# Attention feeding a maxout FFN: immediate activation biases, another path for the first K and Q, and denominators issued apart from numerators

## The chip, the cores and the metric

The kernel runs on one core of a Trainium2 chip. TensorE (PE) multiplies, VectorE (DVE) and ScalarE (ACT) work elementwise, GpSimd (POOL) and SyncE (SP) here mainly issue DMAs. POOL's DMAs can cast fp32 to fp16 on the way. The metric is the device time of one execution in microseconds (us). The kernel before takes 356.96 us, the median of 13 runs from 353.17 to 360.54.

## The reference

```python
scores = (q @ k.T) / sqrt(64)              # q, k, v: 8 batches, 12 heads, 448 x 64
e = exp(scores - max)
attn = e / (sum(e) + exp(-max))            # softmax with one added to the denominator
x = (attn @ v)                             # heads side by side: 3584 x 768
h = maximum(maximum(x @ w1, x @ w2), x @ w3)
out = h @ w_out                            # 3584 x 768, weights 768 x 768
```

## The kernel before

Heads are taken in groups of four: 8 batches times 3 groups are 24 groups, numbered 0 to 23. Matrix work is in fp16. For each group Q and K (two halves of two heads) and V are loaded by POOL with a cast, Q and K are transposed into `qkT`, scores are multiplied into PSUM tiles `stp`, ACT takes their exponential into `eT` (first name `eTp`), a product with ones gives the denominators `den`, ACT makes the reciprocal as `rb = exp(-ln(den + 1/8) + ln 256)` in two ACTIVATEs over `lnd`, a product with V gives the numerators (`num` or `av`), and DVE multiplies both into `xT`, the transposed input of the FFN. A piece of the up-projection multiplies `xT` with one of three weights into `p_i`, and DVE folds it into `hT` with a maximum. The down-projection writes `op_ps`, which DVE scales into `o_sb` and SP stores.

The order is written out by hand. For the start there is a string of operations; from group 4 on a loop issues, per group, scores, the numerators of two groups before, denominators of the group before, and FFN pieces by a credit. The letters of the string that matter: `Cg` cast of the pair for group g, `Tg` both transposes on PE, `Sgp` scores and exponentials of part p (the queries are cut into 3 and 4 blocks of 64), `sgp` the last of them, `Agp` denominators and numerators, `M1` one piece of up-projection, `U V W` the three score visits of a whole group, `X5` copies for group 5 and its transpose by DMA on SP. Groups 1 to 4 are transposed on PE, from 5 on by DMA.

PSUM tiles of two banks (`stp`, `den`) rotate over three buffers and tiles of one bank (`trT`, `num`, `p_i`, `op_ps`) over two; each engine does its instructions in the order given. Group 0's K and Q come as fp32 over the hardware queues of SP and ACT and are cast by DVE. POOL's loads are issued in the order of the calls; each waits for the eighth before it to land, and a tile's load waits until its buffer is free (five for Q and K, six for V). Biases of the ACTIVATEs are [128, 1] tiles that DVE sets once (`e_b`, `one_b`, `ln_lam`).

## Time and profile before

| | us |
|---|---|
| median of 13 runs | 356.96 |
| the profiled execution, whole | 355.06 |
| its span, first to last instruction | 353.3 |
| PE busy | 322.9 |
| DVE busy | 234.7 |
| ACT busy | 205.6 |
| POOL busy | 92.0 |
| first scores on PE | 11.91 |
| first up-projection on PE | 29.32 |
| scores of group 5 on PE, the first that wait for a transpose by DMA | 65.32 |

The profile is one execution. Busy time counts instructions that an engine is at; a busy PE is not PE at its peak. The page gives busy shares in slices, the granted PE clock, DMA traffic and the chain of work that ended last; tables by stage show which engine is full where. What counts for the time is the engine or the transfer that others wait for in a stage. Line numbers (L296) are those of the kernel before.

### The profile page before, as it was taken

Reading aid. Unit: us, or ns where it says so; the run is one execution under the profiler, and the core shown is the slowest. Engines: PE = TensorE matmul, PEld = TensorE weight load, DVE = VectorE, ACT = ScalarE, POOL = GpSimd, SP = SyncE. Lnnn points to the kernel's source line nnn. Section 1 sums busy time; section 2 is a strip of 40 time slices with the busy share of each in tenths; the row PEclk is TensorE's granted clock in tenths of the full one; section 3 lists DMA queues with packets and bytes.
Section 4 is the critical chain, followed back from the end, with each engine's and each line's share of the span. In section 5 each row is a group of like instructions: output and inputs, shape, how many; then the busy total and the mean of one; then the engine's idle time right before and its main releaser. Section 6 shows DMA issues by size and latency. Waiting matters only on the chain.

```text
span 353.3 us, 7731 instructions
## 1 busy us (share of the span) xinstructions
PE 322.9 (91%) x3198; PEld 180.7 (51%) x3198; DVE 234.7 (66%) x434; ACT 205.6 (58%) x226; POOL 92.0 (26%) x158
## 2 busy tenths in 40 slices
PE   0777879799999999999999999999999999899994
PEld 0656757454454554445445555455445544444552
DVE  0422458488677787787786777778777786654553
ACT  1598778588566667659458567566666665420000
POOL 6934957134240440342142143041000000000000
PEclk9999999899999999999999999999999999999999
DMA  8999999979955896598683995578302630022006
GB/s 162 194 209 205 184 202 166 139 113 228 134 90 95 151 186 106 78 121 153 124 126 65 182 186 92 90 125 167 65 8 54 163 70 2 0 66 69 0 4 177
DMA packets 63172, 41.93 MB, mean 119 GB/s; under 512 B 38048, under 2 KB 59552, under 8 KB 63136
## 3 DMA queue, kind: packets, MB, share of 16 engines
q0 software_dynamic: 23424, 20.78, 40.0%
q1 hardware_dynamic: 39424, 20.19, 27.3%
q10 hardware_dynamic: 288, 0.46, 0.6%
q8 instruction: 25, 0.41, 0.5%
q14 instruction: 11, 0.09, 0.1%
HBM read 42.47 MB, written 11.01 MB: 151 GB/s over the span
## 4 chain that ended last, share of the span: by engine, by line
PE 78%; ACT 8%; DMA 6%; DVE 5%; issue 1%; POOL 0%; SPq 0%; DVEq 0%
PE p_i L355 42%; PE op_ps L398 15%; PE av L238 8%; PE stp L198 7%; DVE xT L277 3%; PE p_i L376 3%; ACT eT L216 3%; DMA qkT<-qk 3%; ACT eTp L296 3%; DMA first_k<-in_k_dram 2%; PE den L238 2%; DMA ld_q<-in_q_dram 1%; ACT rb L327 1%; ACT lnd L323 1%; PE trT L168 1%
## 5 line engine op out<-in xcount | busy, mean ns | idle before, releaser
L216 ACT ACTIVATE eT<-stp,e_b 128x896 f16<-128x896 f32 x147 | 136.6, 1008 | 84.6 <-PE stp L198 84.6
L355 PE MATMUL p_i<-xT,w 128*128 128x448 f16 x756 | 148.1, 352 | 3.2 <-DVE xT L277 1.2
L355 PEld LDWEIGHTS <-w 128*128 128x128 f16 x756 | 72.7, 98 | 74.6 <-issue 9.6
L365 DVE TENSOR_TENSOR hT<-hT,p_i 128x448 f16<-128x448 f16 x84 | 52.2, 621 | 30.1 <-PE p_i L355 30.1
L224 DVE TENSOR_TENSOR eS<-eS,eT 128x896 f16<-128x896 f16 x105 | 65.0, 619 | 2.8
L88 POOL DMA_DIRECT2D ld_v<-in_v_dram x48 | 28.7, 609 | 137.7 <-PE stp L198 116.2
L198 PE MATMUL stp<-qkT 64*64 64x448 f16 (+2 forms) x756 | 53.7, 347 | 8.1 <-ACT eT L216 2.3
L398 PE MATMUL op_ps<-w,hT 128*128 128x384 f16 x336 | 57.8, 326 | 0.0
L398 PEld LDWEIGHTS <-hT 128*128 128x128 f16 x336 | 31.7, 98 | 24.6 <-issue 2.5
L405 DVE TENSOR_SCALAR o_sb<-op_ps 128x384 f32<-128x384 f32 x56 | 31.1, 555 | 15.2 <-PE op_ps L398 13.8
L198 PEld LDWEIGHTS <-qkT 64*64 64x64 f16 x756 | 21.4, 109 | 33.8 <-issue 28.1
L363 DVE CAST hT<-p_i 128x448 f16<-128x448 f32 x42 | 26.2, 625 | 17.4 <-PE p_i L355 17.4
L238 PE MATMUL av<-eT,ld_v 64*64 64x448 f16 x588 | 36.9, 362 | 0.9 <-DVE o_sb L405 0.5
L277 DVE TENSOR_TENSOR xT<-av,rb 128x448 f16<-128x448 f32 x42 | 24.3, 620 | 12.1 <-PE av L238 12.0
L238 PEld LDWEIGHTS <-ld_v 64*64 64x64 f16 x756 | 25.7, 108 | 12.8 <-issue 7.6
L88 POOL DMA_DIRECT2D ld_k<-in_k_dram x46 | 28.5, 642 | 5.2 <-DMA w<-in_moe_w_dram 3.3
L88 POOL DMA_DIRECT2D ld_q<-in_q_dram x46 | 28.1, 628 | 4.8 <-DMA w<-in_moe_w_dram 2.9
L296 ACT ACTIVATE eTp<-stp,e_b 128x768 f16<-128x768 f32 (+3 forms) x24 | 20.1, 910 | 11.0 <-PE stp L198 10.8
L257 ACT ACTIVATE lnd<-den,one_b 128x896 f32<-128x896 f32 x21 | 21.2, 1007 | 8.8 <-PE den L238 8.8
L376 PE MATMUL p_i<-xT,w 128*128 128x192 f16 (+1 forms) x216 | 22.8, 259 | 1.2 <-DVE xT L339 0.7
L259 ACT ACTIVATE rb<-lnd,ln_lam 128x896 f32<-128x896 f32 x21 | 21.9, 1042 | 0.7
L376 PEld LDWEIGHTS <-w 128*128 128x128 f16 x216 | 19.1, 98 | 5.4 <-issue 3.3
(36 smaller groups left out, 107.9 us busy)
## 6 DMA issues: line engine op xcount, KB each, us to landing
out_dram<-o_sb SPq DMA_DIRECT2D x56, 192.0 KB, 3.1
ld_v<-in_v_dram POOLq DMA_DIRECT2D x48, 112.0 KB, 4.1
ld_k<-in_k_dram POOLq DMA_DIRECT2D x46, 112.0 KB, 4.9
ld_q<-in_q_dram POOLq DMA_DIRECT2D x46, 112.0 KB, 4.6
w<-in_moe_w_dram POOLq DMA_DIRECT2D x3, 576.0 KB, 10.6
w<-in_moe_w_dram POOLq DMA_DIRECT2D x6, 288.0 KB, 9.8
w<-in_moe_w_out_dram POOLq DMA_DIRECT2D x3, 384.0 KB, 7.5
first_k<-in_k_dram SPq DMA_DIRECT2D x2, 224.0 KB, 6.0
```

The source lines that it names most:

```text
L88: eng.dma_start(out=dst[hp * KC : hp * KC + KC].rearrange("p s j d -> p s (j d)"), in_=src[:, half_heads(name, hp)],)
L198: nc.tensor.matmul(out=out[half(c), r], lhsT=qkT[half(r), 0, j, h], rhs=qkT[half(r), 1, q0:q1, h], start=True, stop=True,)
L216: nc.scalar.activation(out=st["eT"][:, j], in_=stp[:, :, 0:S], func=AF.Exp, scale=scale, bias=e_b)
L224: nc.vector.tensor_tensor(out=st["eS"], in0=st["eT"][:, 0] if j == 1 else st["eS"], in1=st["eT"][:, j], op=ALU.add,)
L238: nc.tensor.matmul(out=outs[r][half(c)], lhsT=weights(r, c), rhs=moving(r, c), start=start, stop=stop,)
L277: nc.vector.tensor_tensor(out=xT[b][:, 2 * g + r, :], in0=banks[r][:, 0:S], in1=st["rb"][:, r], op=ALU.mult)
L296: nc.scalar.activation(out=eT[:, j0 : j0 + n].rearrange("p j r q -> p r j q"), in_=stp[:, :, 0 : n * nq].rearrange("p r (j q) -> p r j q", ...
L355: nc.tensor.matmul(out=p_i[:, 0:S], lhsT=w_sb[i][:, dc, ts(fc, 128)], rhs=xT[b][:, dc, :], start=(dc == 0), stop=(dc == NDC - 1),)
L365: nc.vector.tensor_tensor(out=dst, in0=dst, in1=p_i[:, 0:S], op=ALU.max)
L376: nc.tensor.matmul(out=p_i[:, ts(j, nq)], lhsT=w_sb[i][:, dc, ts(2 * fp + j, 128)], rhs=xT[b][:, dc, q0 * KC : q1 * KC], start=(dc == 0), ...
L398: nc.tensor.matmul(out=op_ps[:, 0:NW], lhsT=hT[bp][:, fc, ts(t, 128)], rhs=wout_sb[:, fc, ts(nh, NW)], start=(fc == 0), stop=(fc == NFC - 1),)
L405: nc.vector.tensor_scalar(out=o_sb[:, ts(nh, NW)], in0=op_ps[:, 0:NW], scalar1=1.0 / LAMBDA, scalar2=None, op0=ALU.mult,)
```

## The change

- The three bias tiles and their memsets go; the ACTIVATEs take their biases as numbers in the instruction.
- Group 0's K comes in two halves, one on SP's and one on ACT's hardware queue. Group 0's Q is loaded by POOL's casting queue, first of POOL's loads, and is transposed like the other groups' (14 transposes of 64 rows in place of 7). Q's cast on DVE goes.
- POOL builds the identity ahead of group 1's loads instead of behind them. Among later loads the third weight goes ahead of group 3's K and Q, and group 3's V ahead of group 4's K and Q.
- V has five buffers instead of six.
- In the start, scores are issued one PSUM tile at a time (`Sgpu`, unit u), and `A` is split into `D` (denominators with the two ACTIVATEs) and `N` (numerators and the product on DVE), in another order.

```diff
-                [128, 2, NJ, D], MMDT, tag="ld_" + name, name="ld_" + name, bufs=6 if name == "v" else 5
+                [128, 2, NJ, D], MMDT, tag="ld_" + name, name="ld_" + name, bufs=5
...
-    first = {}
-    for name, eng in (("k", nc.sync), ("q", nc.scalar)):
-        first[name] = cpool.tile([128, 2, NJ, D], FP32, name="first_" + name)
-        for hp in range(2):
-            load_half(eng, first[name], name, 0, hp)
-    load_group(1, "kq")
+    first_k = cpool.tile([128, 2, NJ, D], FP32, name="first_k")
+    load_half(nc.sync, first_k, "k", 0, 0)
+    load_half(nc.scalar, first_k, "k", 0, 1)
+    load_group(0, "q")
     ident16 = cpool.tile([128, 128], MMDT, name="ident16")
     make_identity(nc, ident16)
+    load_group(1, "kq")
...
-            if i == 0:
+            if i == 0 and n == 0:
...
-                out=st["eT"][:, j], in_=stp[:, :, 0:S], func=AF.Exp, scale=scale, bias=e_b
+                out=st["eT"][:, j], in_=stp[:, :, 0:S], func=AF.Exp, scale=scale, bias=-math.log(EDIV)
...
+    load_weight(2)
     load_group(3, "kq")
-    load_weight(2)
+    load_group(3, "v")
     load_group(4, "kq")
-    load_group(3, "v")
...
-        C0 T0 S00 T1 s00 S10 T2 s10 A00 S20 A10 s20 S01 A20 s01
-        S11 M1 s11 M1 M1 A01 S21 M1 s21 M1 T3 M1 A11 U3 M1 A21 V3 T4 E30 M1 M1 W3 E31 X5 F
+        C00 T0 S000 S001 S002 T1 S003 S100 S101 D00 T2 S102 S103 N00 S200 S201 D10 S202 S203 N10
+        S010 D20 S011 S012 N20 S013 M1 M1 S110 D01 S111 N01 S112 S113 M1 M1 S210 D11 S211 N11
+        S212 S213 M1 T3 M1 D21 M1 U3 N21 T4 V3 E30 M1 M1 W3 E31 X5 F
```

What POOL's queue holds first, before (the names end in buffer numbers; ld_k_97 and ld_q_100 are group 1's, ld_v_108 is group 0's V):

```order
L88 DMA ld_k_97<-in_k_dram 64x2x448 x2
L88 DMA ld_q_100<-in_q_dram 64x2x448 x2
masks.py:197 MEMSET ident16_103 128x128
masks.py:199 ISA
masks.py:199 AFFINE_SELECT ident16_103<-ident16_103 128x128
L88 DMA ld_v_108<-in_v_dram 64x2x448 x2
```

And in the changed kernel (ld_q_94 is group 0's Q, ld_k_102 and ld_q_105 group 1's):

```order
L88 DMA ld_q_94<-in_q_dram 64x2x448 x2
masks.py:197 MEMSET ident16_97 128x128
masks.py:199 ISA
masks.py:199 AFFINE_SELECT ident16_97<-ident16_97 128x128
L88 DMA ld_k_102<-in_k_dram 64x2x448 x2
L88 DMA ld_q_105<-in_q_dram 64x2x448 x2
L88 DMA ld_v_108<-in_v_dram 64x2x448 x2
```

Group 0's Q has come in front, and group 1's K and Q have moved behind the identity.

ACT up to the third reciprocal, before (eTp 128x2x2x192 and 128x384 are exponentials of part 0, 128x2x2x256 of part 1):

```order
L296 ACTIVATE eTp<-stp,e_b 128x2x2x192 x3
L296 ACTIVATE eTp<-stp,e_b 128x384
L296 ACTIVATE eTp<-stp,e_b 128x2x2x192 x3
L296 ACTIVATE eTp<-stp,e_b 128x384
L323 ACTIVATE lnd<-den,one_b 128x2x192
L327 ACTIVATE rb<-lnd,ln_lam 128x2x192
L296 ACTIVATE eTp<-stp,e_b 128x2x2x192 x3
L323 ACTIVATE lnd<-den,one_b 128x2x192
L327 ACTIVATE rb<-lnd,ln_lam 128x2x192
L296 ACTIVATE eTp<-stp,e_b 128x384
L296 ACTIVATE eTp<-stp,e_b 128x2x2x256 x3
L323 ACTIVATE lnd<-den,one_b 128x2x192
```

And the end of the same stretch in the changed kernel, from the second reciprocal on:

```order
L307 ACTIVATE lnd<-den 128x2x192
L311 ACTIVATE rb<-lnd 128x2x192
L284 ACTIVATE eTp<-stp 128x2x2x192
L284 ACTIVATE eTp<-stp 128x384
L284 ACTIVATE eTp<-stp 128x2x2x256
L307 ACTIVATE lnd<-den 128x2x192
L311 ACTIVATE rb<-lnd 128x2x192
L284 ACTIVATE eTp<-stp 128x2x2x256 x2
```

The bias operands are gone, and one exponential of part 1 stands ahead of the third pair `lnd`, `rb` where there were three.

## The prediction

> **What bounds the kernel now.** I read the page's busy shares first, then a table of the engines by stage, then the chain that ended last over the first 60 us, the waits of PE, and single rows where a price was needed. Columns of the stage table: stretch, length, busy us (instructions) of PE, weight loads, DVE, ACT, POOL, then granted PE clock, DMA share, GB/s.

> ```profile
> span 353.3 us, 7731 instructions
> PE 322.9 (91%) x3198; PEld 180.7 (51%) x3198; DVE 234.7 (66%) x434; ACT 205.6 (58%) x226; POOL 92.0 (26%) x158
> ...
> 0.00:10.00 10.00, 0.48 (x5) 0.48 (x6) 1.30 (x6) 1.28 (x1) 7.34 (x17) 1.00 0.88 167
> 10.00:20.00 10.00, 8.87 (x204) 7.53 (x202) 3.76 (x7) 7.00 (x10) 7.51 (x13) 1.00 1.19 197
> 20.00:30.00 10.00, 6.08 (x186) 4.39 (x177) 1.87 (x6) 9.94 (x15) 4.39 (x8) 1.00 1.18 207
> 30.00:40.00 10.00, 9.56 (x178) 8.05 (x177) 4.69 (x9) 7.62 (x9) 6.19 (x11) 1.00 1.20 198
> 40.00:50.00 10.00, 8.14 (x194) 7.03 (x192) 3.86 (x10) 7.21 (x9) 6.25 (x11) 1.00 1.16 193
> 60.00:100.00 40.00, 36.43 (x346) 20.56 (x346) 29.07 (x55) 27.84 (x31) 10.69 (x18) 0.96 0.96 144
> 100.00:150.00 50.00, 49.51 (x427) 25.48 (x421) 38.81 (x73) 33.63 (x36) 14.26 (x24) 1.00 0.71 122
> ```

> The reader is to see three limits. From 100 us on PE has work for 49.5 of each 50 us: nothing off PE can gain there. From 20 to 30 us ACT is busy 9.94 of 10 and PE waits for it. Before 10 us nothing computes, and DMA is full at about 200 GB/s until past 50 us. So the change can only act in the first 65 us or so, and the chain there says where:

> ```profile
> 1.56 7.18 DMA first_k<-in_k_dram
> ...
> 8.84 0.64 DVE qk L147
> ...
> 9.52 1.69 PE trT L162 x14
> ...
> 11.23 0.64 DVE qkT L171
> ...
> 11.91 1.18 PE stp L198 x24
> ...
> 55.77 9.51 DMA qkT<-qk
> ```

> The first scores start at 11.91 because the second half of the first K lands at 8.74. At 55.77 the chain goes through the first DMA transpose (group 5).

> **The change, part by part.** *First loads.* Before, SP issues both K halves, ACT both Q halves, all fp32; POOL's first load is group 1's K.

> ```profile
> 0.74 1.65 SPq L88 DMA_DIRECT2D first_k<-in_k_dram  x2
> 0.77 1.37 ACTq L88 DMA_DIRECT2D first_q<-in_q_dram  x2
> 1.25 1.32 POOL L88 DMA_DIRECT2D ld_k<-in_k_dram  x2 [0.80 <-POOLq L570]
> 2.54 1.22 POOL L88 DMA_DIRECT2D ld_q<-in_q_dram  x2
> ...
> DMA to landing us min/median/max: 4.9/6.0/7.2
> DMA to landing us min/median/max: 3.9/4.8/5.7
> DMA to landing us min/median/max: 4.9/5.7/6.6
> ...
> ld_k<-in_k_dram POOLq DMA_DIRECT2D x46, 112.0 KB, 4.9
> first_k<-in_k_dram SPq DMA_DIRECT2D x2, 224.0 KB, 6.0
> ...
> 13.77 0.96 PE L168 MATMUL trT<-ident,ld_q 128*64 128x128 f16 x14
> ```

> The three landing rows are those of first_k, first_q and the first two ld_k. The 7.2 is the second K half, so SP's first landed at 0.74 + 4.9 = 5.64 and ACT's first at 0.77 + 3.9 = 4.67. In the changed kernel K's halves are these two firsts: K is there at 5.64. With the gaps of the chain (0.10 to the cast, 0.68 to the transposes, half of 1.69 for 7 of 14) K's transposes end at 7.26. Q now takes the place of ld_k: halves at 1.25 + 4.9 = 6.15 and about 1.97 + 6.6 = 8.57. Its 14 narrower transposes take 0.96, the copy 0.64, hand-overs 0.14. If Q is there by 7.26 the scores start at 8.95 (gain 2.97); at 8.57, at 10.3 (gain 1.6). Q's second half then no longer shares with 0.46 MB of fp32 Q, but still with K; I take 7.6, scores at 9.34: **-2.6**, ends -3.0 and -1.6. Three DVE memsets and one DVE cast go at a time when DVE only waits for K: nothing.

> POOL now builds the identity after Q, so group 1's K and Q are issued some 1.9 us later, where ld_q and ld_v stood. Rows like ld_q's (2.54, 3.16, landing 6.3) put their last half near 10.6. They are wanted at 10.5 and 11.4: the wait is 0 to 0.2, taken as 0. If that cover is gone (first scores before 9), it eats what was gained beyond.

> *Order of the first groups.* ACT sets the pace until the first up-projection:

> ```profile
> 12.50 3.17 ACT L296 ACTIVATE eTp<-stp,e_b 128x768 f16<-128x768 f32 x4 [10.47 <-PE stp L198]
> ...
> 23.65 3.58 ACT L296 ACTIVATE eTp<-stp,e_b 128x384 f16<-128x384 f32 x4
> 27.10 0.59 ACT L323 ACTIVATE lnd<-den,one_b 128x384 f32<-128x384 f32 x1
> 27.73 0.61 ACT L327 ACTIVATE rb<-lnd,ln_lam 128x384 f32<-128x384 f32 x1
> ...
> 29.32 1.16 PE L376 MATMUL p_i<-xT,w 128*128 128x192 f16 x12
> ```

> The chain to p_i is ACT back to back from 12.50 to rb's end at 28.34, then xT and PE. The row at 23.65 holds one exponential of 384 and three of part 1 (1024 wide); ahead of the third reciprocal the new order keeps one of the three. Two go: (3.58 - 0.52) / 3 = 1.02 each, -2.04. Against it stands a new ACT gap: T2 is put ahead of S102, and group 1's exponentials wait for it, taken as 0.45 (after S101 PE needs about 3.1 at the early rows' pace for denominators, transposes and S102; ACT has about 2.65 to do). Net **-1.6** (ends -2.0 and -0.6). The two exponentials are done later, where ACT is 7.6 and 7.2 of 10 busy: hidden while that slack of 5.2 stands. From 30 to 50 PE is idle 0.44 + 1.86 = 2.3; much of it stands behind numerators whose reciprocal comes late, and denominators issued earlier should take some: **-0.5** (ends 0 and -1.8). The same nine pieces of up-projection are issued by the end of the start, so behind it the program is unchanged.

> *Immediates.* Each ACTIVATE loses the read of a [128,1] bias. No row has an immediate, so bound it:

> ```profile
> L216 ACT ACTIVATE eT<-stp,e_b 128x896 f16<-128x896 f32 x147 | 136.6, 1008 | 84.6 <-PE stp L198 84.6
> ...
> 51.29 6.39 ACT L216 ACTIVATE eT<-stp,e_b 128x896 f16<-128x896 f32 x7 [2.52 <-PE stp L198]
> ```

> One takes 1008 ns, seven in a row 913 each: 95 ns already lie under the predecessor. Between lnd's 590 ns for 384 elements (row 27.10) and 1008 for 896 an element costs 0.82, so 180 ns of the 913 are no elements. The lower end is no gain; the upper, that all 180 go in each of the 18 ACTIVATEs up to the third reciprocal: 3.2. I take 95 ns for those with no predecessor to lie under (three rb behind their lnd, two or three first ones): about **-0.5**, nearest to the row of seven, which hides the rest. Later PE is the bound.

> [...]

> *Weights and V.* Weight 3 goes ahead of group 3's K and Q, so these land later by its 1.18 MB, 5.9 us at 200 GB/s, less 1.2 for group 0's Q that is cast (0.23 MB less).

> ```profile
> 20.41 0.59 POOL L88 DMA_DIRECT2D ld_q<-in_q_dram  x1 [0.89 <-DMA w<-in_moe_w_dram]
> ...
> DMA to landing us min/median/max: 9.4/9.9/10.4
> ...
> 38.10 0.58 PE L168 MATMUL trT<-ident,ld_k 128*64 128x128 f16 x14
> ...
> 40.48 0.96 PE L238 MATMUL den<-eTp,ones 64*64 64x256 f16 x28
> ```

> Group 3's last Q half landed at 20.41 + 9.4 = 29.8, now 34.5. Its transposes stood at 38.10; less 5.2, and with group 1's second denominators (0.96) and as much of numerators now ahead of them, they stand near 34.8: no wait, end +1.5. One V buffer fewer makes POOL wait for the numerators one group later. POOL idles in steady state before ld_v in any case:

> ```profile
> POOL ld_v L88 <- PE stp L198: 116.2, 13, 11.3
> ...
> PE stp L198 <- DMA qkT<-qk: 2.2, 1, 2.2
> ```

> Behind that wait in POOL's queue stand the K and Q that are copied two groups on, over 20 us; they land within 10: 0.

> *The first DMA transpose.* PE waits 2.2 us for it up to 65.3, and the clock then falls:

> ```profile
> 66.00:67.00 1.00, 1.00 (x16) 0.58 (x12) 0.00 (x0) 1.00 (x2) 0.00 (x0) 0.50 1.14 69
> 68.00:69.00 1.00, 1.00 (x16) 0.47 (x12) 0.05 (x1) 0.56 (x1) 0.00 (x0) 0.50 0.57 126
> ```

> Half clock from about 65.9 to 69.2 costs some 1.7 us. The transpose is issued behind PE-paced copies, so it moves forward with PE, and loads are still in flight then: its 9.5 us stay, and so do wait and dip: 0 (ends -3.9 and +4.0).

> Sum: -2.6 - 1.6 - 0.5 - 0.5 = **-5.2**. The profiled execution took 355.06 (span 353.3 and 1.76 around it): 349.9. It lies 1.9 under the median of 356.96, so a median is **351.8**.

> **The rivals.** (A) The sum as it stands: 351.8, by itself 350.3 to 353.4; chance 0.42. (B) With V's loads of group 8 and the K and Q behind them held back until the numerators of group 3, DMA is freer in 56 to 65 and the transpose lands in time: a further -2.2 - 1.7, 347.9. Against it: PE comes 5 us earlier, into the loads that are left. 0.13. (C) DMA is full, so the transpose cannot land earlier than its bytes allow: PE arrives early and waits longer, and only the 0.23 MB that no longer go ahead (1.2 us) remain: 355.8. 0.14. (D) All 18 exponentials and reciprocals gain 95 ns: 350.6. 0.10. (E) The K halves share the same bandwidth, so two queues save only the issue of one half, 0.8 us of SP: the scores start 0.7 earlier, -3.3 in all, 353.7. For it: DMA is full from 3 us on; against: both first halves landed 2 to 3 us ahead of the second. 0.12.

> [...]

> (F) Slower: group 3's Q lands so late behind weight 3 that PE stands at its transposes. It decides when it lands 5.2 us after 34.8, at 40.0: the 6.3 MB up to it (0.46, ten casts of 0.23, three weights of 1.18) in the 38 us since loads began would be 166 GB/s, where the table shows 193 to 207. At 41.5, with a dip of 1.7 behind so long a wait, 360.2. 0.09.

> **How the numbers follow.** Within 0.5% (1.8 us), which is about what a measurement of this kernel can tell from no change, lie C and the slow edges of A and E (0.05): 0.19. Slower is F, 0.09; faster the rest, 0.72. The range leaves out half of B and F with the edge of C, under 0.2: 347.6 to 356.4.

> **What would show it.** First scores at about 9.3 (not 11.9), K's cast at 5.7; first p_i near 24 to 25 (not 29.3); eT at 1008 - 95 = 913 alone, and 913 again in a row of seven (D: 820); group 3's transposes without a DMA wait; the wait for the first qkT by DMA still near 2.2 with a clock of 0.50 behind it, now near 60. The forecast is wrong if the first scores move and the end of that wait does not (C), or if it is gone (B).

## The result and the profile after

The changed kernel takes 348.89 us (median of 11 runs, 347.46 to 350.0) against 356.43 us before (48 runs, 353.09 to 361.86): a ratio of 0.980, 95% interval 0.977 to 0.983, so 7.5 us less. The profiled execution of the changed kernel took 351.78 us, more than any of the 11 others; the one of before, at 355.06, is 1.4 us under its median. So the two traces differ by 3.3 us where the medians differ by 7.5, and the traces alone do not account for the result.

The top of the page after, then the table by stage, with the columns of the one before:

```profile
span 350.0 us, 7739 instructions
...
PE 319.5 (91%) x3205; PEld 180.5 (52%) x3205; DVE 234.0 (67%) x430; ACT 186.1 (53%) x226; POOL 93.0 (27%) x160
```

```profile
0.00:10.00 10.00, 3.28 (x53) 2.69 (x55) 2.10 (x4) 2.16 (x3) 8.88 (x20) 1.00 0.89 149
10.00:20.00 10.00, 7.64 (x226) 6.38 (x226) 3.03 (x6) 7.53 (x13) 6.47 (x11) 1.00 1.13 181
20.00:30.00 10.00, 7.05 (x204) 6.09 (x192) 2.36 (x6) 7.57 (x12) 3.60 (x6) 1.00 1.16 210
...
100.00:150.00 50.00, 49.13 (x432) 25.45 (x431) 39.12 (x73) 29.17 (x35) 12.85 (x23) 1.00 0.71 124
```

ACT has lost 19.5 us of busy time over the span. From 100 us on PE is busy 49.1 of 50, close to the 49.5 of before, so none of that counts there. From 20 to 30 us ACT is at 7.57 of 10, no longer 9.94, and PE still only at 7.05: something other than ACT holds it. The chain that ended last (start, duration) says what:

```profile
0.74 4.44 DMA first_k<-in_k_dram
...
5.20 0.75 DVE qk L139
...
8.54 1.18 PE stp L186 x24
...
17.24 1.68 issue
...
25.64 2.14 PE p_i L371 x24
...
52.00 10.41 DMA qkT<-qk
```

The scores start at 8.54 instead of 11.91, 3.4 us earlier, and the first up-projection at 25.64 instead of 29.32, 3.7 earlier. Between them stands a link that the earlier chain did not have: 1.68 us of "issue", in which PE waits for nothing that the profile names. The waits of PE, with total, times and longest in us, list it with a second one, and the old wait for the first DMA transpose is longer, not shorter:

```profile
PE stp L186 <- DMA qkT<-qk: 3.2, 1, 3.2
...
PE den L226 <- issue: 1.7, 1, 1.7
PE num L226 <- issue: 1.4, 1, 1.4
```

Each run also lists the granted clock, as a mean over the execution. In the trace of before it is 0.994: 3.4 us at 0.50 behind the transpose take 0.005 off, and 0.75 us at 0.50 after PE's last product, where it costs nothing, the rest. That end at half clock is 0 to 3.3 us long in the traces here, so the mean sorts runs only roughly: the profiled `imm_only`, at 0.991, has one stretch and a long end. Sorted by it, the runs of the kernel before that were taken beside the experiments, and the 12 of the changed kernel (runs over 1.5% above the fastest are left out, 12 of before and none of after):

| mean granted clock | before: runs, median us | after: runs, median us |
|---|---|---|
| 0.997 to 1.000 (no stretch of half clock) | 12, 354.1 | 5, 348.1 |
| 0.992 to 0.996 (one, as a rule) | 20, 356.0 | 7, 349.4 |
| 0.991 and less (two, or one and a long end) | 25, 357.6 | none |

At a like clock the change is worth 6.0 and 6.6 us. The rest of the 7.5 is fewer stretches of half clock: 25 of 57 runs of before lie in the lowest row, none of the 12 after. Both profiled executions are of the middle row.

### The profile page after: what moved, and what is told of

Read it like the earlier page. It is cut to its first block, busy times and chain, and to the rows that moved or that the text cites. A ratio compares the mean times of both kernels' runs of the same rounds, so it can differ in the third digit from the quotient of the medians.

```text
span 350.0 us, 7739 instructions
## 1 busy us (share of the span) xinstructions
PE 319.5 (91%) x3205; PEld 180.5 (52%) x3205; DVE 234.0 (67%) x430; ACT 186.1 (53%) x226; POOL 93.0 (27%) x160
## 3 DMA queue, kind: packets, MB, share of 16 engines
q0 software_dynamic: 23712, 21.01, 41.5%
## 4 chain that ended last, share of the span: by engine, by line
PE 78%; ACT 7%; DVE 7%; DMA 4%; issue 2%; DVEq 0%
PE p_i L350 42%; PE op_ps L393 15%; PE stp L186 7%; PE av L226 6%; PE p_i L371 4%; ACT eT L204 4%; DVE xT L265 4%; DMA qkT<-qk 3%; PE den L226 2%; ACT eTp L284 1%; PE trT L156 1%; DMA first_k<-in_k_dram 1%; DVE eS L212 1%; DVE qkT L159 1%; DVE o_sb L400 1%
## 5 line engine op out<-in xcount | busy, mean ns | idle before, releaser
L204 ACT ACTIVATE eT<-stp 128x896 f16<-128x896 f32 x147 | 123.5, 924 | 99.5 <-PE stp L186 99.5
L88 POOL DMA_DIRECT2D ld_v<-in_v_dram x48 | 28.8, 616 | 141.5 <-PE stp L186 137.4
L186 PE MATMUL stp<-qkT 64*64 64x448 f16 (+2 forms) x756 | 51.3, 346 | 6.1 <-DMA qkT<-qk 3.2
L186 PEld LDWEIGHTS <-qkT 64*64 64x64 f16 x756 | 20.7, 109 | 27.5 <-issue 20.6
L88 POOL DMA_DIRECT2D ld_k<-in_k_dram x46 | 28.3, 637 | 11.0 <-DMA ld_q<-in_q_dram 3.4
L88 POOL DMA_DIRECT2D ld_q<-in_q_dram x48 | 29.2, 627 | 4.6 <-DMA w<-in_moe_w_dram 3.0
L284 ACT ACTIVATE eTp<-stp 128x768 f16<-128x768 f32 (+3 forms) x24 | 18.4, 818 | 11.5 <-PE stp L186 11.4
L245 ACT ACTIVATE lnd<-den 128x896 f32<-128x896 f32 x21 | 19.4, 925 | 9.1 <-PE den L226 9.1
L247 ACT ACTIVATE rb<-lnd 128x896 f32<-128x896 f32 x21 | 20.0, 952 | 0.7
## 6 DMA issues: line engine op xcount, KB each, us to landing
ld_q<-in_q_dram POOLq DMA_DIRECT2D x48, 112.0 KB, 4.3
ld_v<-in_v_dram POOLq DMA_DIRECT2D x48, 112.0 KB, 4.3
ld_k<-in_k_dram POOLq DMA_DIRECT2D x46, 112.0 KB, 4.4
```

The costliest lines, as they stand in the source:

```text
L88: eng.dma_start(out=dst[hp * KC : hp * KC + KC].rearrange("p s j d -> p s (j d)"), in_=src[:, half_heads(name, hp)],)
L186: nc.tensor.matmul(out=out[half(c), r], lhsT=qkT[half(r), 0, j, h], rhs=qkT[half(r), 1, q0:q1, h], start=True, stop=True,)
L204: nc.scalar.activation(out=st["eT"][:, j], in_=stp[:, :, 0:S], func=AF.Exp, scale=scale, bias=-math.log(EDIV))
```

## The experiments

**Each part alone, put into the kernel before.** These four are compared with runs of before at 356.27.

Biases as immediates (`imm_only`), the same at all six ACTIVATE lines:

```diff
-    e_b = cpool.tile([128, 1], FP32, name="e_b")
-    nc.vector.memset(e_b, -math.log(EDIV))
...
-                out=st["eT"][:, j], in_=stp[:, :, 0:S], func=AF.Exp, scale=scale, bias=e_b
+                out=st["eT"][:, j], in_=stp[:, :, 0:S], func=AF.Exp, scale=scale, bias=-math.log(EDIV)
```

> The kernel before with immediates for the biases and nothing else. My sum's theory (the bias read lies under the predecessor when ACT is back to back): -0.5 us, 0.999 of before, and eT in a row of seven still 913 ns apart. Rival (each ACTIVATE gets 93 ns shorter, in a row as well, as the row of seven in the changed kernel suggests with 4.13 us for five): -1.7 us up to the third reciprocal and up to -3 in all, 0.992 to 0.995, eT near 820 ns apart.

353.43 us, ratio 0.994 (0.990 to 0.999): by the ratio 2.0 us, with 0.5 to 3.5 inside the interval. Its group of exponentials (the first line) shows one at 923 ns instead of 1008, 85 less. Whether the saving holds behind a predecessor is read from the changed kernel, from its group (the second line) and its timeline (start, duration of five in a row):

```profile
L210 ACT ACTIVATE eT<-stp 128x896 f16<-128x896 f32 x147 | 123.4, 923 | 97.5 <-PE stp L192 97.5
...
L204 ACT ACTIVATE eT<-stp 128x896 f16<-128x896 f32 x147 | 123.5, 924 | 99.5 <-PE stp L186 99.5
```

```profile
73.24 4.13 ACT L204 ACTIVATE eT<-stp 128x896 f16<-128x896 f32 x5
```

Five take 4.13 us, 826 each, where seven took 913 each before: the 87 ns go in a row too. By shape, an ACTIVATE of the changed kernel is 82 to 97 ns shorter than its like before: `lnd` of 896 elements 925 instead of 1007, `lnd` of 384 elements 494 instead of 587 (93 less), exponentials of 1024 elements 1014 instead of 1111. That is what rival D assumed.

The new path of the first K and Q (`first_only`), with the start's order as it was:

```diff
-    first = {}
-    for name, eng in (("k", nc.sync), ("q", nc.scalar)):
...
-    load_group(1, "kq")
+    first_k = cpool.tile([128, 2, NJ, D], FP32, name="first_k")
+    load_half(nc.sync, first_k, "k", 0, 0)
+    load_half(nc.scalar, first_k, "k", 0, 1)
+    load_group(0, "q")
     ident16 = cpool.tile([128, 128], MMDT, name="ident16")
     make_identity(nc, ident16)
+    load_group(1, "kq")
...
```

> The kernel before with group 0's K on both hardware queues, its Q by the casting queue and the identity ahead of group 1's loads, nothing else. My sum's theory: the first scores start 2.6 to 3.4 us earlier (8.5 to 9.3 instead of 11.9), and the time follows: -2.6 to -3.4, 0.991 to 0.993. Rival (DMA takes it back at the first transpose of group 5, which can land no earlier than its bytes allow): the scores start as early, the wait for that transpose grows from 2.2 to 4 or 5, and the time moves by -1.2 at most, 0.997.

354.72 us, 0.993 (0.988 to 0.998): 2.4 us, with 0.6 to 4.3 in the interval. Its timeline (start, duration, in brackets the wait ahead):

```profile
8.55 1.17 PE L197 MATMUL stp<-qkT 64*64 64x192 f16 x24 [0.72 <-DVE qkT L170]
...
20.90 0.61 PE L237 MATMUL den<-eTp,ones 64*64 64x192 f16 x20 [3.13 <-issue]
...
64.72 0.76 PE L197 MATMUL stp<-qkT 64*64 64x448 f16 x12 [2.50 <-DMA qkT<-qk]
```

The scores stand where the whole change has them, so this part alone brings the 3.4 us, and 3.1 us are then spent in a wait of the kind "issue" before 20.90. That wait costs a second time: right behind it, from 21.6 to 25.0 us, PE is at half clock (0.83 over the ten us, the third figure from the end).

```profile
20.00:30.00 10.00, 7.42 (x180) 6.10 (x181) 1.68 (x5) 8.38 (x12) 3.71 (x7) 0.83 1.18 207
```

The traces of `imm_only`, `all_but_order` and `pause` have such a stretch in the start too (from 21.9, 20.7 and 26.4 us); so a stretch of half clock is not always the transpose's.

The new order of the start (`order_only`): scores by tile, denominators apart, with `C01` added since Q is still cast by DVE.

```diff
-        C0 T0 S00 T1 s00 S10 T2 s10 A00 S20 A10 s20 S01 A20 s01
-        S11 M1 s11 M1 M1 A01 S21 M1 s21 M1 T3 M1 A11 U3 M1 A21 V3 T4 E30 M1 M1 W3 E31 X5 F
+        C00 C01 T0 S000 S001 S002 T1 S003 S100 S101 D00 T2 S102 S103 N00 S200 S201 D10 S202 S203 N10
+        S010 D20 S011 S012 N20 S013 M1 M1 S110 D01 S111 N01 S112 S113 M1 M1 S210 D11 S211 N11
+        S212 S213 M1 T3 M1 D21 M1 U3 N21 T4 V3 E30 M1 M1 W3 E31 X5 F
```

> The kernel before with the new order of the start alone (denominators apart from numerators, scores by units), old loads, old order of weights, pointer biases, six V buffers. My sum's theory: -1.6 to -2.1 us, 0.994 to 0.9955, the first p_i about 1.6 us earlier. Rival (the order gives the first p_i earlier and loses it again later in the start, where the exponentials that were put off are done): 0 to -0.5, 0.999 to 1.0.

358.31 us, 1.004 (0.999 to 1.009): no gain. The timeline:

```profile
22.52 0.32 PE L233 MATMUL den<-eTp,ones 64*64 64x192 f16 x5 [1.68 <-issue]
...
28.64 2.15 PE L378 MATMUL p_i<-xT,w 128*128 128x192 f16 x24
...
67.64 1.33 PE L193 MATMUL stp<-qkT 64*64 64x448 f16 x12 [4.64 <-DMA qkT<-qk]
```

The up-projection comes 0.7 us earlier, not 1.6, behind a wait of 1.68, and the transpose is waited for 4.64 us instead of 2.2.

Five V buffers (`v5_only`):

```diff
-                [128, 2, NJ, D], MMDT, tag="ld_" + name, name="ld_" + name, bufs=6 if name == "v" else 5
+                [128, 2, NJ, D], MMDT, tag="ld_" + name, name="ld_" + name, bufs=5
```

> The kernel before with five V buffers instead of six, nothing else. My sum's theory: 0, ratio 1.0. Rival (group 8's V and group 9's K and Q are held back behind group 3's numerators, DMA is freer from 56 to 65 us and group 5's transpose lands in time): -2 to -4 us, 0.989 to 0.994, the wait of 2.2 us for that transpose gone and with it the half clock behind it.

356.03 us, 0.997 (0.992 to 1.001): the time alone does not tell it from nothing. Its profiled execution took 351.17, 3.9 less than the one of before, and there the stage from 60 to 70 us and the landing of group 5's transpose read:

```profile
60.00:70.00 10.00, 9.80 (x118) 7.05 (x116) 7.98 (x16) 7.93 (x10) 3.57 (x6) 1.00 0.67 111
```

```profile
DMA to landing us min/median/max: 6.3/6.3/6.3
```

PE at 9.80 instead of 7.64, clock 1.00 instead of 0.83, and a landing in 6.3 us instead of 9.5: that is rival B in a trace. Five of its 12 runs have a clock of 0.997 or more; of the kernel before, 12 of 69. These five have a median of 354.4, against 354.1 in the table's first row: at a like clock the removal of the sixth buffer brings nothing, so what it can bring is fewer stretches.

**Without the transpose that PE waits for.** Group 5's pair transposed by PE, in the kernel before (`pe6_before`) and in the changed one (`pe6_after`); the edit is the same:

```diff
-    PE_TR = 5
+    PE_TR = 6
...
-        S11 M1 s11 M1 M1 A01 S21 M1 s21 M1 T3 M1 A11 U3 M1 A21 V3 T4 E30 M1 M1 W3 E31 X5 F
+        S11 M1 s11 M1 M1 A01 S21 M1 s21 M1 T3 M1 A11 U3 M1 A21 V3 T4 E30 M1 M1 W3 E31 F
```

> The kernel before, with group 5 transposed by PE as well, so no group waits for a DMA transpose early on. If that wait (2.2 us) and the half clock behind it (1.7 us) are most of what scatters from run to run, the runs lie closer together (before: 353.2 to 360.7 here) and the time falls by 2.2 + 1.7 - 1.2 of PE's transposes, -2.7 us, 0.9925. Rival: the scatter comes from elsewhere (PE's instruction supply in the start); spread as before, and -1 us or less.

> The changed kernel, with group 5 transposed by PE as well. If the changed kernel's usual run no longer pays for the transpose by DMA (its profiled run is the slowest of twelve and does pay 3.2 us and the half clock), this gives nothing or loses PE's 1.2 us: about 349 to 350. If the usual run still pays: 346 to 347. Against the kernel before 0.970 to 0.983.

Beside a kernel before at 356.23: 352.91 us, 0.992 (0.989 to 0.995), and 348.30, 0.978 (0.974 to 0.982). In neither trace does PE wait for a DMA transpose early on. To the kernel before this is worth 2.9 us by the ratio, to the changed one about 0.6 against its 348.89, which the intervals do not tell from nothing; in both, PE pays about 1.2 us for its own 28 transposes (14 take 0.58, below). Between the two 4.6 us remain: that is what the change brings when no DMA transpose is waited for early on. Five of the 12 runs and three of the six still lie at 0.992 to 0.996, so one stretch of half clock comes without that wait.

**Six V buffers in the changed kernel** (`all_but_v5`), the edit of `v5_only` the other way round.

> The changed kernel with six V buffers again. Theory now: with six, POOL runs three loads further ahead, they are in flight when group 5 is transposed by DMA, that transpose lands late and PE stands and goes to half clock: 351 to 353, 0.986 to 0.991 of before, so five buffers are worth 2 to 4 us inside the changed kernel. My sum's theory: no difference from the changed kernel, 349, 0.98.

351.78 us, 0.986 (0.981 to 0.991): 2.2 us slower than the changed kernel by the ratios, 2.9 by the medians, though the intervals just touch (0.983 and 0.981). The timeline at the wait, the stage and a single us of the end of the slow stretch:

```profile
62.46 1.33 PE L186 MATMUL stp<-qkT 64*64 64x448 f16 x12 [3.94 <-DMA qkT<-qk]
```

```profile
60.00:70.00 10.00, 7.50 (x71) 4.47 (x72) 2.61 (x5) 4.26 (x5) 5.13 (x9) 0.66 1.34 169
...
66.00:67.00 1.00, 1.00 (x16) 0.19 (x6) 0.49 (x1) 0.17 (x1) 0.25 (x1) 0.50 1.25 123
```

The wait is 3.94 us and the half clock lasts 6.8 us of these ten (0.34 / 0.5): two stretches in a row. Five of its six runs have a clock of 0.991 or less, none of the 12 of the changed kernel. So here the removed V buffer goes with fewer stretches. It is not enough by itself: of the kernels below that also have five buffers, `pause` has three of four runs at 0.991 or less, `all_but_imm` and `all_but_order` three of six each. Nor do the two traces show how it helps: group 5's transpose lands in 10.4 us with five buffers and in 11.1 with six.

**What "issue" is.** The stall stands before the 222nd matmul in 11 and before the 350th in 13 of the 14 traces, whatever these matmuls do. Before: at 21.78 and 27.70, where the table of PE's own instructions has 221 by 21.70.

```profile
21.78 0.49 PE L238 MATMUL den<-eTp,ones 64*64 64x192 f16 x13 [0.16 <-issue]
27.70 0.70 PE L198 MATMUL stp<-qkT 64*64 64x256 f16 x17 [0.97 <-issue]
```

```profile
0.00:21.70 21.70, 10.05 (x221) 1.00 1.05 184
```

In the changed kernel, PE's own instructions from the start, to the beginning and into the first stall, and to the second:

```profile
0.00:17.30 17.30, 9.85 (x221) 1.00 0.98 159
0.00:18.00 18.00, 9.85 (x221) 1.00 0.99 161
0.00:24.80 24.80, 13.23 (x349) 1.00 1.03 174
```

```profile
18.93 0.44 PE L226 MATMUL den<-eTp,ones 64*64 64x192 f16 x12 [1.68 <-issue]
24.85 0.28 PE L226 MATMUL num<-eTp,ld_v 64*64 64x192 f16 x4 [1.43 <-issue]
```

The two are 128 matmuls apart, with their 128 weight loads 256 instructions. The page's DMA queues (packets, MB, share) have two of instructions. One, q14 with 11 packets of 8 KB, brings none between the start of the span and 53 us, before and in the changed kernel. The other:

```profile
q8 instruction: 25, 0.41, 0.5%
```

0.41 MB in 25 packets are 16 KB each, 64 bytes for each of 256 instructions. So the queue seems to bring PE's instructions in blocks of 256. The theory: PE runs out of instructions, because the next block comes through DMA engines that are full of loads. A test that adds DMA quiet and takes nothing away: POOL, which issues the loads, first fills a weight's buffer with zeros (`pause`).

```diff
+    nc.gpsimd.memset(w_sb[0], 0.0)
     load_weight(0)
```

> The changed kernel with a memset of 4608 elements per partition on POOL ahead of the first weight's load, some 5 us in which POOL issues nothing, so that DMA runs dry about 15 to 20 us. PE stands 1.7 us at its 222nd matmul and 1.4 at its 350th with nothing that it waits for. Theory: its next 128 pairs of instructions (16 KB) have not come, since their fetch shares the full DMA engines; then the first of these waits shrinks to under 0.5 us, and stays at the 222nd matmul if anything is left of it. Rival (PE waits for a buffer or an engine that the profile doesn't name): the wait stays 1.5 to 2 us. The time as a whole may go either way, 347 to 352, since the weights come later.

351.74 us, 0.987 (0.982 to 0.993). The fill took 4.01 us. The stage, PE's own instructions past the place of the first stall, and the waits:

```profile
10.00:20.00 10.00, 8.45 (x264) 6.78 (x264) 3.65 (x8) 9.11 (x17) 9.70 (x11) 1.00 0.83 118
```

```profile
0.00:17.30 17.30, 9.66 (x237) 1.00 0.83 134
```

```profile
PE num L226 <- issue: 1.8, 1, 1.8
```

With the DMA share from 10 to 20 us at 0.83 instead of 1.13, PE is at 237 matmuls by 17.30, where it stood at 221: of the first stall 0.10 us is left. The second, behind the quiet, stays at 1.8. The execution is slower all the same: its loads come later, it waits 2.35 us for group 5's transpose, and two stretches are at half clock.

The trace also keeps the time of every packet of the instruction queue, 16,384 bytes each. Its first two packets beside the two matmuls (us from the span's start):

| trace | first packet lands | 222nd matmul | PE had stood | second lands | 350th matmul | PE had stood |
|---|---|---|---|---|---|---|
| changed kernel | 17.69 | 18.93 | 1.68 | 23.60 | 24.85 | 1.43 |
| `first_only` | 19.42 | 20.90 | 3.13 | 25.52 | 26.82 | 0.94 |
| `pause` | 15.67 | 16.99 | 0.10 | 22.13 | 23.46 | 1.81 |
| `pair` (below) | 16.32 | 19.71 | none | 24.17 | 25.63 | none |

In all 14 traces, wherever there is such a stall, it ends 1.2 to 1.5 us after a packet has landed. That shows what PE waits for: its instructions. The first packet starts 1.95 us after the 94th matmul, with which the block before begins, in `pause`, and 2.2 to 6.0 after it in the 13 others. From 75 us on, where DMA is less full (0.76 in the changed kernel from 75 to 150 us, instead of 1.1 to 1.2 from 10 to 60), most packets start before the block ahead of theirs begins: 11 of 17 in the changed kernel, 12 of 18 before. The packet itself takes 0.9 to 1.6 us in these two traces, the first one 1.21 and 0.95. When a block is asked for the trace does not say, so that the loads hold it up is inferred from these starts.

**One part taken back from the changed kernel**, beside a kernel before at 357.72. With bias tiles (`all_but_imm`), with the old order of the start (`all_but_order`), and with the old path of the first K and Q (`all_but_first`); each is the edit above the other way round.

> The changed kernel with the biases in tiles again. The edit alone gave 0.9944 (0.990 to 0.9986) on the kernel before. Theory (immediates shorten every ACTIVATE of the start by 90 ns, in a row too, and ACT paces part of the start): 1 to 2 us slower than the changed kernel, 350 to 351, 0.983 to 0.986 of before. Rival (my sum's: they save next to nothing, PE's instruction supply and the loads set the start): as the changed kernel, 0.980.

> The changed kernel with the old order of the start (denominators and numerators together), all else new. The order alone gave 1.004 (0.999 to 1.009) on the kernel before. Theory now: the order is worth little, since PE's 222nd and 350th matmuls come no earlier than their instructions: 348 to 350.5, 0.978 to 0.984. My sum's theory: 2.1 us slower than the changed kernel, 351, 0.986.

> The changed kernel with group 0's K and Q as before (fp32 over two queues, K's halves both on SP, group 1's loads first on POOL). Theory: the first scores are 3.4 us later, and of that 1.5 to 3 us show in the time, the rest being waited at the 222nd and 350th matmul anyway: 350.5 to 352, 0.984 to 0.988. My sum's theory: all of it shows, 351.5 to 352.3, 0.986 to 0.989. The two overlap; what tells them apart are the two waits without a named cause: under 1 us together here, against 3.1 in the changed kernel's profile.

352.19 us, 0.982 (0.975 to 0.988); 351.35, 0.982 (0.977 to 0.987); 352.62, 0.989 (0.985 to 0.993). The first is inconclusive: its six runs spread from 348.08 to 359.38. The second is not told from the changed kernel's 0.980: the order is worth nothing that can be measured. The third costs 0.9%, 3.3 us. The waits of the last two, which tell how much of a part the instruction stall takes:

```profile
19.95 0.61 PE L231 MATMUL den<-eTp,ones 64*64 64x192 f16 x20 [2.44 <-issue]
...
27.30 1.17 PE L369 MATMUL p_i<-xT,w 128*128 128x192 f16 x12
```

```profile
11.84 1.18 PE L187 MATMUL stp<-qkT 64*64 64x192 f16 x24 [0.71 <-DVE qkT L160]
...
21.40 0.32 PE L227 MATMUL den<-eTp,ones 64*64 64x192 f16 x5 [1.36 <-issue]
...
27.32 0.27 PE L187 MATMUL stp<-qkT 64*64 64x256 f16 x1 [1.38 <-issue]
...
63.94 0.76 PE L187 MATMUL stp<-qkT 64*64 64x448 f16 x12 [2.79 <-DMA qkT<-qk]
```

With the old order the stall is 2.44 and the up-projection at 27.30. With the old first loads the two stalls are 2.7 together, where the expectation had under 1: a later start alone does not make them go. The wait for group 5's transpose is 2.79 us in this trace, and no half clock follows.

**Fewer instructions ahead of the stall** (`pair`): in the changed kernel DVE copies K and Q of groups 1 and 2 into pairs, so that 7 transposes of 128 rows each do for 14 of 64, and group 5 is transposed by PE.

```diff
-            if i == 0 and n == 0:
+            if i in (1, 2) or (i == 0 and n == 0):
...
-        C00 T0 S000 S001 S002 T1 S003 S100 S101 D00 T2 S102 S103 N00 S200 S201 D10 S202 S203 N10
+        C00 T0 C10 C11 S000 S001 S002 T1 S003 S100 S101 D00 C20 C21 T2 S102 S103 N00 S200 S201 D10 S202 S203 N10
```

> The changed kernel with group 5 transposed by PE and with the K and Q of groups 1 and 2 paired on DVE, so that PE transposes them in 7 instructions each instead of 14: 28 matmuls and as many weight loads fewer ahead of the third group's denominators. If PE's instructions come in blocks of 128 matmuls with their weight loads, waits without a named cause stand again at the 222nd and the 350th matmul, which are now 28 matmuls later in the work, and the work ahead of them is done some 1 to 1.5 us sooner: 346.5 to 347.8, 0.973 to 0.977. Rival (DVE's four copies of 0.4 us come into the chain from K's and Q's landing to the scores, or the instruction count doesn't matter): 348 to 349.

346.96 us, 0.973 (0.969 to 0.977): the fastest here, 1.3 us under `pe6_after`, though their intervals overlap. Its timeline:

```profile
8.54 1.18 PE L186 MATMUL stp<-qkT 64*64 64x192 f16 x24 [0.72 <-DVE qkT L159]
...
23.98 2.14 PE L371 MATMUL p_i<-xT,w 128*128 128x192 f16 x24 [0.40 <-DVE xT L334]
```

The up-projection stands at 23.98. The time is the expected one, the sign is not: the waits were to stand again at the 222nd and the 350th matmul, and no "issue" is left among the waits of PE. The table of packets says why. With 28 matmuls and 28 weight loads fewer, each boundary of 256 instructions comes later in the work; the 222nd matmul runs at 19.71, well behind its packet, and the 350th 1.46 us after its own, just late enough not to wait. Which of the savings brought the time (less PE work, fewer instructions, no wait for group 5's transpose) was not taken apart and stays open.

## Why the prediction was right, and where its steps were not

The forecast was 351.8 us, by itself 350.3 to 353.4; the time is 348.89, inside the stated range and 1.4 under that inner one, nearest to rival B's 347.9. The sum of 5.2 stands against 6.0 to 6.6 at a like clock. Its terms did worse than its total, and that the total came so near is luck: the order, 2.1 of the 5.2, brought nothing that could be measured, while the first loads, the immediates and the V buffer brought more than they were given.

- **First loads, -2.6: right in kind, a little small.** K was cast at 5.20 (5.7 foreseen) and the scores started at 8.54 (9.34), so 3.4, beyond the end of 3.0. Alone the part is worth 2.4 us, and taken back it costs 3.3. Rival E, that the halves share one bandwidth, is out.
- **Order of the first groups, -1.6 and -0.5: wrong.** This is the step that failed. The forecast counted exponentials ahead of the third reciprocal on ACT and put a row of PE work behind them, as if PE always had its instructions. ACT did fall to 7.57 of 10, and p_i came at 25.64 where 24 to 25 was foreseen; but PE stood 3.1 us for instructions, and in `order_only` longer at the transpose. Alone 1.004, taken back not to be told from nothing.
- **Immediates, -0.5: wrong in size.** The step took from the row of seven that 95 ns already lay under the predecessor. In a row 826 instead of 913 was measured. Alone it brought 2.0 us (0.5 to 3.5); in the changed kernel its share is open, since `all_but_imm` is inconclusive. The traces have 82 to 97 ns less for one ACTIVATE, by shape; rival D's 95 ns, over the 18 that the prediction counts 1.7 us, lie near the 2.0. (The ACTIVATEs up to the third reciprocal are 19, not 18; that changes it by 0.1.)
- **Weight 3 and group 3's Q, 0: right in the trace.** Group 3's transposes show no wait for a DMA in the timeline, though 2.4 us later than foreseen, as PE itself was late; the order of these loads was not tried by itself.

```profile
37.16 0.58 PE L156 MATMUL trT<-ident,ld_k 128*64 128x128 f16 x14
```

- **One V buffer fewer, 0: too small.** The forecast looked at what stands behind the wait in POOL's queue and found it early enough. It did not ask what that leaves free: loads that come later can make room for group 5's transpose, which landed in 6.3 us in `v5_only` against 9.5 before. The price in `all_but_v5` is 2.2 to 2.9 us, at the edge of what its six runs can tell, and the profiled changed kernel does not show the mechanism (10.4 us).
- **The first DMA transpose, 0: right for the profiled execution, open for the usual one.** In the profiled one the wait is 3.2 us and 3.4 us at half clock follow. But by the clock five runs in 12 have no half clock ahead of PE's end and none lies in the lowest row, where 25 of 57 did; and taking that transpose away gains nothing that can be measured in the changed kernel. That the wait is short in the usual run is inferred from this; no trace of such a run was taken, and up to some 1.8 us could hide behind the 1.2 that PE's own transposes cost. So the time lies nearest to B's 347.9 without B's mechanism having been seen in the changed kernel.

Nothing moved where PE is full, as foreseen: the first and the last of the products with 448 columns into `p_i` both come 3.6 us earlier (84.7 instead of 88.3 and 336.6 instead of 340.2). F, group 3 late, did not happen; C, that DMA takes it all back, holds for the profiled execution in part and not for the median.

## What to carry to other kernels

A gain in the start is worth what the first fixed arrival behind it lets through: here a transpose that competes with loads (it landed in 9.5 us before, in 6.3 in `v5_only`), and the fetch of PE's instructions, which came late while the DMA engines were full (a first stall of 1.68 us at a DMA share of 1.13, of 0.10 at 0.83 in `pause`). So ask of each step what it takes off the DMA engines at that moment, and count the matmuls ahead of a stall that has no named cause: if it stands at the same count in every variant (221 and 349 here), the instruction queue's packets tell whether it is the fetch (PE went on 1.2 to 1.5 us after one had landed). A stretch of half clock behind such a stall or wait cost another 1.3 to 1.9 us here, by the medians of the table of clocks.

One profiled execution can lie at the edge of its runs (351.78 us here, the 11 others 347.46 to 350.0). The granted clock listed with every run tells cheaply, if roughly, which kind it was, and edits should be compared at a like clock. A buffer more may not be free where its early load stands in the way of something that is waited for: with the sixth for V, `all_but_v5` took 2.2 to 2.9 us more.
